# VectorE transposes that write contiguously, with the token order and the head masks made afterwards by ScalarE and GpSimd

## Chip, cores and metric

One core of a Trainium2 chip runs the kernel. The metric is device time in microseconds (us), the median of the runs. Before the change the kernel took 167.43 us (two runs, 166.48 and 168.37). A profile shows one execution. Fast runs of the kernel before differ by up to 1.4% within one set of rounds, so differences of 1 or 2 us between single traces are read with care, and the experiments were timed in several rounds against the kernel before on the same chip.

Engine names in the profile: PE is TensorE's matmul part, DVE is VectorE, ACT is ScalarE, POOL is GpSimd, SP issues DMAs. L203 is line 203 of that kernel's source; the changed kernel has other line numbers.

## The reference

A chunked linear attention (state space) layer is followed by a gated feed-forward network (FFN). What matters here, per batch entry and head:

```python
cum = np.cumsum(log(a))                    # decay
y_t = sum_{s<=t} (C_t . B_s) * exp(cum_t - cum_s) * x_s
# shapes: x (4, 8, 768, 32), a (4, 8, 768), B and C (4, 8, 768, 16)
X = y.transpose(0, 2, 1, 3).reshape(3072, 256)
out = (maximum(X @ w_gate, 0) * (X @ w_val)) @ w_out     # w: 256x1536, 256x1536, 1536x256
```

The kernel folds the decay into B and C: C is multiplied by a running product, B by its inverse. TensorE then needs the scaled B and C with the state dimension on the partitions and the tokens along the free axis. They arrive the other way round, so they have to be transposed.

## The kernel before

A batch entry has 768 tokens, split as 32 rows `r` of `K = 24` tokens. Partition p holds four groups (`q`) of 32 rows. Two heads (`t = 0, 1`) share a group, 16 state values each. The load puts B and C as `[(q r), t, (k n)]`, so a VectorE transpose of 32x32 blocks turns, for each k, the rows r into 32 columns. Token number is `24 r + k`, so the 32 columns of one block belong 24 elements apart. The kernel writes them there straight from the transpose:

```python
BT = [glob.tile([128, S], BF16) for b in range(NB)]
CT = [glob.tile([128, 2, S], BF16) for b in range(NB)]
bq = [glob.tile([128, K, 2 * N], BF16) for b in range(NB)]
cq = [glob.tile([128, K, 2, 2 * N], BF16) for b in range(NB)]   # C once per head, the other head zero

def turn_b(b, k0=0, k1=K):
    nc.vector.transpose(BT[b].rearrange("p (r k) -> p k r", k=K)[:, k0:k1], bq[b][:, k0:k1])

def turn_c(b, t, k0=0, k1=K):
    nc.vector.transpose(CT[b][:, t].rearrange("p (r k) -> p k r", k=K)[:, k0:k1],
                        cq[b][:, k0:k1, t])
```

Batch entry 0 is prepared in the start, before any FFN work. Entries 1, 2 and 3 are prepared inside FFN blocks 0, 1 and 2, between the products of the FFN (a block is 512 tokens, 12 slices f of the FFN width; the first four are done in two halves, `gvh`):

```python
for f in range(4, NF):
    gv(b, f)            # 4 matmuls, relu on ScalarE -> r, h = r * val on VectorE
    ... prep(step)      # steps 0, 1: scale B and C on GpSimd
                        # steps 2..4: turn_b in thirds;  5..10: turn_c in thirds, two heads
# after gv: state products, then fout (y @ w_out) in four quarters, with G = C.B of the next pair between
```

In the traces every engine takes its instructions in the order of the program. Six PSUM banks are shared by the FFN products and G, and a `gv` takes two of them, so PE can run about three slices ahead of VectorE.

Of the kernel before, what the change touches and what calls it, by code (L numbers as in the profile page):

```python
# [9 lines left out]
BF16 = mybir.dt.bfloat16  # L10
AF = mybir.ActivationFunctionType
ALU = mybir.AluOpType
# [17 lines left out]
def kernel(  # L30
# [13 lines left out]
    nc = tc.nc  # L44

    NB, NH, S, D = x.shape
    N = B.shape[-1]
# [7 lines left out]
    R = 32  # L55
    K = S // R
# [3 lines left out]
    glob = ctx.enter_context(tc.tile_pool(name="glob", bufs=1))  # L60
# [7 lines left out]
    def bank(name="bank", shape=(128, 512), dtype=FP32):  # L68
        return mm.tile(list(shape), dtype, tag="shared", bufs=NSHARED, name=name)
# [4 lines left out]
    def load_rows(src, b, q, name):  # L74
        rows = glob.tile([128, 2, K * N], FP32, name="%s%d" % (name, b))
        q.dma_start(out=rows, in_=src[b].rearrange("(t q) (r k) n -> (q r) t (k n)", t=2, r=R))
        return rows
# [12 lines left out]
    rows = {}  # L90
# [21 lines left out]
    tmask = const.tile([128, 2], FP32)  # L112
# [23 lines left out]
    def weights(f0, f1):  # L136
        fs = slice(f0 * 128, f1 * 128)
        for w, src in ((wg, moe_w_gate), (wv, moe_w_val)):
            nc.gpsimd.dma_start(
                out=w[:, :, fs], in_=src[:, fs].rearrange("(k p) f -> p k f", k=2))  # L140
# [8 lines left out]
    def wait_for(j, cell):  # L149
        nc.gpsimd.tensor_copy(gate[:, j:j + 1], cell)  # L150


    FC = const.tile([128, 2 * NB, K], FP32)
    FB = const.tile([128, 2 * NB, K], FP32)
# [20 lines left out]
    def inverse(b):  # L175
        nc.vector.reciprocal(FB[:, 2 * b:2 * b + 2], FC[:, 2 * b:2 * b + 2])
# [3 lines left out]

    BT = [glob.tile([128, S], BF16, name="BT%d" % b) for b in range(NB)]
    CT = [glob.tile([128, 2, S], BF16, name="CT%d" % b) for b in range(NB)]
    bq = [glob.tile([128, K, 2 * N], BF16, name="bq%d" % b) for b in range(NB)]
    cq = [glob.tile([128, K, 2, 2 * N], BF16, name="cq%d" % b) for b in range(NB)]

    def clear(b, eng):
        for t in range(2):
            eng.memset(cq[b][:, :, t, (1 - t) * N:(2 - t) * N], 0.0)

    def scale_c(b, t, eng):  # L190
        eng.tensor_tensor(
            out=cq[b][:, :, t, t * N:(t + 1) * N],
            in0=rows["C", b][:, t].rearrange("p (k n) -> p k n", n=N),
            in1=FC[:, 2 * b + t].to_broadcast([128, K, N]), op=ALU.mult)

    def scale_b(b, t, eng):
        eng.tensor_tensor(  # L197
            out=bq[b][:, :, t * N:(t + 1) * N],
            in0=rows["B", b][:, t].rearrange("p (k n) -> p k n", n=N),
            in1=FB[:, 2 * b + t].to_broadcast([128, K, N]), op=ALU.mult)  # L200

    def turn_b(b, k0=0, k1=K):
        nc.vector.transpose(BT[b].rearrange("p (r k) -> p k r", k=K)[:, k0:k1], bq[b][:, k0:k1])  # L203

    def turn_c(b, t, k0=0, k1=K):
        nc.vector.transpose(CT[b][:, t].rearrange("p (r k) -> p k r", k=K)[:, k0:k1],  # L206
                            cq[b][:, k0:k1, t])

    yT = glob.tile([128, 2, T], BF16)
    A_ps = mm.tile([128, 2, 128], FP32, tag="Aps", name="A_ps")  # L210
# [8 lines left out]
    def tokens(p, i):  # L219
        c = 2 * (p % PPB) + i  # L220
        return slice(c * 128, (c + 1) * 128)

    def rows_b(p):
        s = st[p]
        n = 1 if 2 * (p % PPB) + 1 == NC - 1 else 2
        bb = bank("bb", (128, 2, 128), BF16)
        for i in range(n):
            nc.tensor.transpose(out=bb[:, i], in_=BT[p // PPB][:, tokens(p, i)], identity=ident)
        bt = att.tile([128, 2, 128], BF16, tag="bt", name="bt")
        nc.scalar.copy(out=bt[:, 0:n], in_=bb[:, 0:n])  # L230
        s["B"] = [bt[:, i] for i in range(n)]

    def G(p):
        s = st[p]
        b = p // PPB
        g = [bank("g%d" % q, (128, 2, 2, 128)) for q in range(4)]
        for i in range(2):
            for q in range(4):
                r = slice(32 * q, 32 * q + 32)
                nc.tensor.matmul(  # L240
                    out=g[q][:, i], lhsT=BT[b][r, tokens(p, i)], rhs=CT[b][r, :, tokens(p, i)],
                    start=(i == 0), stop=True, tile_position=(32 * q, 0),
                    skip_group_check=True)
        s["gp"] = g
        s["gs"] = att.tile([128, 4, 4, 128], BF16, tag="gs", name="gs", bufs=2)
# [75 lines left out]
    def yevac(p, eng):  # L321
        s = st.pop(p)
        dst = yT[:, :, p * 256:(p + 1) * 256]
        src = s["y"].rearrange("r t i m -> r t (i m)")
        if eng is nc.scalar:
            eng.copy(out=dst, in_=src)  # L326
        else:
            eng.tensor_copy(dst, src)
# [59 lines left out]

    factors(0, 2)
    inverse(0)  # L390
    clear(0, nc.gpsimd)
    wait_for(0, al[0:1, 0, 1:2])
    weights(0, 4)
    scale_b(0, 0, nc.vector)
    scale_c(0, 0, nc.gpsimd)
    scale_b(0, 1, nc.vector)
    scale_c(0, 1, nc.vector)
    load_x(1, nc.sync)
    turn_b(0)
    cast_x(0, nc.scalar)  # L400
    keep_warm(10)
    rows_b(0)
    turn_c(0, 0)
    turn_c(0, 1)
    astep(0, 0)
    G(0)
    sevac(0, 0)
    gevac(0, half=False)
    wait_for(1, st[1]["xr"][0:1, 1, 0, 0:1])
# [6 lines left out]
    inter(0, 1)  # L416
    astep(0, 1)
    yevac(0, nc.scalar)
    rows_b(1)
    cast_x(1, nc.scalar)  # L420
    sevac(0, 1)

    for b in range(NBLK):
        P, Q, W = 2 * b + 2, 2 * b + 3, 2 * b + 1
        more = P < NPAIR
        for n in (P + 1, P + 2):
            if n < NPAIR:
                load_x(n, nc.sync)
        if b in (1, 2):
            for j, src in (("B", B), ("C", C)):  # L430
                rows[j, b + 1] = load_rows(src, b + 1, nc.sync, j.lower() + "r")

        def at(name, *fs):

            return more and f == fs[min(b, len(fs) - 1)]

        def prep(step):
            n = b + 1
            if n >= NB:
                return  # L440
            if step < 2:
                scale_b(n, step, nc.gpsimd)
                scale_c(n, step, nc.gpsimd)
            elif step < 5:
                k = 8 * (step - 2)
                turn_b(n, k, k + 8)
            elif step < 11:
                t, k = divmod(step - 5, 3)
                turn_c(n, t, 8 * k, 8 * k + 8)

        for f in range(4):
            gvh(b, f, 0)
            if b == 0 and f == 0:
                G(1)
                gevac(1)
                state(1, 0)
                weights(8, NF)
                wait_for(2, st[2]["xr"][0:1, 1, 0, 0:1])
                weights_out(0, NF)
                clear(1, nc.gpsimd)  # L460
            if f == (3 if b == 0 else 1):
                if b == 1:
                    state(W, 1)
                inter(W, 0)
                inter(W, 1)
                Dm(W)
                if b == 0:
                    state(1, 1)
                yevac(W, nc.scalar)
        for f in range(4):  # L470
            gvh(b, f, 1)
        for f in range(4, NF):
            if b == 0 and f == 4:
                factors(2, 8)
                for n in range(1, NB):
                    inverse(n)
            gv(b, f)
            if f == 4 and b in (1, 2):
                clear(b + 1, nc.gpsimd)
            if f in (4, 5):  # L480
                prep(f - 4)
            if f >= 6:
                prep(f - 4)
            if at("cast P", 6, 4, 4):
                cast_x(P, nc.gpsimd)
            if at("cast Q", 8, 5, 4):
                cast_x(Q, nc.gpsimd)
            if at("rows P", 7, 6, 5):
                rows_b(P)
            if at("state P0", 9, 8, 7):  # L490
                state(P, 0)
            if at("state P1", 10, 10, 9):
                state(P, 1)
            if at("rows Q", 99, 9, 8):
                rows_b(Q)
        if more:
            inter(P, 0)
            inter(P, 1)
        fout(b, 0)
        prep(8)  # L500
        foevac(b, 0)
        if more:
            G(P)
            gevac(P)
        prep(9)
        prep(10)
        if b == 0:
            rows_b(Q)
        fout(b, 1)
        foevac(b, 1)  # L510
        if more and b > 0:
            state(Q, 0)
        fout(b, 2)
        foevac(b, 2)
        if more:
            Dm(P)
            yevac(P, nc.scalar)
            G(Q)
            gevac(Q)
            state(Q, 1 if b else 0)  # L520
        fout(b, 3)
        foevac(b, 3)
# [32 lines left out]
```

## Time and profile before

| stretch (us) | what | PE's idle |
|---|---|---|
| 0 to 21.8 | start: loads, batch 0 prepared, first pair's attention | half |
| 21.8 to 52.3, 52.3 to 79.9, 79.9 to 111.0 | blocks 0, 1, 2: FFN plus preparation of batches 1, 2, 3 | 5.6 to 8.2 us each |
| 111.0 to 167.7 | blocks 3, 4, 5: FFN without preparation | none until the tail |

Blocks are cut where their first FFN matmul starts. The next lines are the engine-busy view of these stretches: for each stretch its length, then busy time and instructions of each engine, PE's granted clock (1.00 is full), and the DMA share and rate.

```profile
core 0: us, PE busy (x) PEld busy (x) DVE busy (x) ACT busy (x) POOL busy (x), PEclk, DMA share, GB/s
0.00:21.80 21.80, 11.32 (x54) 4.28 (x55) 17.95 (x37) 4.14 (x8) 7.42 (x19) 0.73 0.87 161
21.80:52.30 30.50, 22.76 (x183) 13.79 (x183) 27.02 (x48) 13.21 (x29) 10.95 (x20) 0.89 0.47 70
52.30:79.90 27.60, 22.04 (x175) 13.92 (x173) 21.20 (x32) 12.24 (x26) 6.14 (x11) 0.84 0.28 68
79.90:111.00 31.10, 22.94 (x176) 13.96 (x175) 25.43 (x40) 12.36 (x26) 8.30 (x15) 0.86 0.24 60
111.00:129.90 18.90, 18.90 (x176) 12.75 (x174) 12.32 (x24) 12.33 (x26) 1.94 (x4) 0.97 0.28 58
```

Block 3 takes 18.9 us and PE is busy in all of it. Blocks 0 to 2 take 28 to 31 us with the same FFN work. VectorE is busy for 21 to 27 us in them, and 12.3 us in block 3: the transposes of the preparation alone are 11.2 to 12.1 us of it in each of the three blocks. PE itself is busy 22.0 to 22.9 us there and 18.9 in block 3, at a granted clock of 0.84 to 0.89 against 0.97; so besides 5.6 to 8.2 us of idle time each block has 3 to 4 us in which PE is busy longer. In the start VectorE is busy for 17.95 of 21.8 us.

The groups of instructions by shape (busy us, mean ns of one, then idle time before them and its cause) show what that surplus is made of:

```profile
L206 DVE STREAM_TRANSPOSE CT<-cq 128x256 bf16<-128x256 bf16 x18 | 22.9, 1403 | 0.0
...
L203 DVE STREAM_TRANSPOSE BT<-bq 128x256 bf16<-128x256 bf16 x9 | 12.0, 1331 | 7.1 <-POOL bq L197 7.1
...
L206 DVE STREAM_TRANSPOSE CT<-cq 128x768 bf16<-128x768 bf16 x2 | 7.4, 3894 | 0.0
...
L203 DVE STREAM_TRANSPOSE BT<-bq 128x768 bf16<-128x768 bf16 x1 | 3.7, 3690 | 0.0
```

A transpose of 256 columns takes 1.33 to 1.40 us, one of 768 takes 3.7 to 3.9 us: (3690 - 1331) / 512 = 4.6 ns a column. That is over four cycles at the 0.96 GHz that the Trainium skill gives for this engine ("VectorE: DVE Perf Modes", section "Specifications"). Per batch the transposes take 11 us or more.

The chain of waits in the start (start us, duration, what) runs through them:

```profile
6.97 3.61 DVE BT L203
10.59 7.05 DVE CT L206 x2
17.68 0.62 PE g L240 x7
```

The first G matmul (`g`) waits from about 10.6 to 17.7 us for the two C transposes. In block 1 the timeline of VectorE (start, duration, instruction, and in brackets the idle time before it and its cause) shows two things:

```profile
64.48 1.35 DVE L203 STREAM_TRANSPOSE BT<-bq 128x256 bf16<-128x256 bf16 x1 [3.35 <-POOL bq L197]
65.45 0.89 DVE L345 TENSOR_TENSOR h<-r,val 128x512 bf16<-128x512 bf16 x1
66.27 1.32 DVE L203 STREAM_TRANSPOSE BT<-bq 128x256 bf16<-128x256 bf16 x1
67.21 0.90 DVE L345 TENSOR_TENSOR h<-r,val 128x512 bf16<-128x512 bf16 x1
```

and PE's timeline shows what it waits for in the meantime:

```profile
69.65 0.37 PE L276 MATMUL A_ps<-xb,bt 128*128 128x256 bf16 x1 [3.90 <-DVE Sm L284]
```

First, VectorE idles 3.35 us until GpSimd has scaled B. That scaling had itself waited 8.6 us for the B load. Second, from then on each h product (`h<-r,val`) is followed by a transpose that takes longer than the product, and PE idles 3.90 us for `Sm`, the evacuation of a state product, which stands behind them in VectorE's queue.

### The profile page before, as it was taken

To read this page: it belongs to the slowest core of one execution; us is meant where nothing else is said; L and a number is where in the kernel's file an instruction comes from. 1 tells how busy PE (TensorE), PEld (TensorE's weight loads), DVE (VectorE), ACT (ScalarE), POOL (GpSimd) and SP (SyncE) were. 2 spreads that over 40 slices of the span, in tenths; PEclk is the share of its full clock that TensorE was granted. 3 is DMA by queue.
4 is the path that set the end of the run, shared out by engine and by line. 5 is a ranking of instruction groups with operands and counts; after the bars stand their busy time and mean duration, and the time that the engine had idled before them with its cause. 6 is when DMAs were issued, how large, how long until landed. Compare 5 with 4: busy or idle time off the path is not lost.

```text
span 167.7 us, 2899 instructions
## 1 busy us (share of the span) xinstructions
PE 132.6 (79%) x1062; PEld 82.3 (49%) x1062; DVE 127.3 (76%) x222; ACT 76.0 (45%) x160; POOL 38.6 (23%) x73
## 2 busy tenths in 40 slices
PE   6810797881959974399894696499999999999992
PEld 2300255331637732167661245377467846786481
DVE  6999557999985746999881999947866778468821
ACT  3100285541224863015682223338745875388610
POOL 7300447460204036002308202301003210220000
PEclk9965569998795999659999579969999999999999
DMA  5999287930010950001590000109002500120012
GB/s 164 203 182 253 35 124 103 170 47 0 0 66 30 173 175 0 0 4 65 110 240 28 0 0 0 65 32 160 0 0 68 121 4 4 37 88 4 0 51 74
DMA packets 34685, 12.07 MB, mean 72 GB/s; under 512 B 26480, under 2 KB 34672, under 8 KB 34672
## 3 DMA queue, kind: packets, MB, share of 16 engines
q1 hardware_dynamic: 29888, 8.75, 23.2%
q0 software_dynamic: 3184, 2.36, 10.2%
q10 hardware_dynamic: 1600, 0.79, 1.7%
q8 instruction: 8, 0.13, 0.3%
q14 instruction: 5, 0.04, 0.1%
HBM read 11.11 MB, written 3.15 MB: 85 GB/s over the span
## 4 chain that ended last, share of the span: by engine, by line
PE 45%; DVE 27%; POOL 8%; DMA 7%; issue 6%; SPq 3%; ACT 2%; POOLq 0%; DVEq 0%; ACTq 0%
PE o L368 15%; DVE CT L206 13%; PE gate L338 7%; PE gv L356 7%; PE val L341 7%; DVE BT L203 5%; DMA br<-in_B_dram 5%; DVE h L345 4%; SPq L84 3%; POOL bq L197 2%; PE g L240 2%; PE y L313 2%; PE A_ps L276 2%; DMA al<-in_a_dram 1%; PE w L128 1%
## 5 line engine op out<-in xcount | busy, mean ns | idle before, releaser
L344 ACT ACTIVATE r<-gate 128x512 bf16<-128x512 f32 x48 | 28.7, 598 | 26.1 <-PE gate L338 22.0
L368 PE MATMUL o<-wo,h 128*128 128x256 bf16 x288 | 39.2, 294 | 1.5 <-DVE h L345 1.5
L345 DVE TENSOR_TENSOR h<-r,val 128x512 bf16<-128x512 bf16 x48 | 34.8, 728 | 5.4 <-ACT r L344 5.4
L368 PEld LDWEIGHTS <-h 128*128 128x128 bf16 x288 | 29.3, 104 | 10.0 <-issue 3.2
L338 PE MATMUL gate<-yT,wg 128*128 128x512 bf16 x96 | 30.4, 400 | 0.6 <-DVE h L345 0.6
L206 DVE STREAM_TRANSPOSE CT<-cq 128x256 bf16<-128x256 bf16 (+1 forms) x20 | 30.4, 1652 | 0.0
L341 PE MATMUL val<-yT,wv 128*128 128x512 bf16 x96 | 30.2, 398 | 0.1
L247 POOL TENSOR_SCALAR_AFFINE_SELECT gs<-gs 128x512 bf16<-128x512 bf16 (+1 forms) x24 | 12.2, 531 | 76.9 <-ACT gs L258 76.9
L360 DVE TENSOR_TENSOR h<-r,gv 128x256 bf16<-128x256 bf16 x48 | 19.9, 421 | 11.4 <-ACT r L359 10.9
L203 DVE STREAM_TRANSPOSE BT<-bq 128x256 bf16<-128x256 bf16 (+1 forms) x10 | 15.7, 1567 | 7.1 <-POOL bq L197 7.1
L264 DVE TENSOR_TENSOR gs<-g,maskUT 128x512 bf16<-128x512 f32 x24 | 16.0, 710 | 6.3 <-PE g L240 3.2
L359 ACT ACTIVATE r<-gv 128x256 bf16<-128x256 f32 x48 | 18.5, 384 | 3.8 <-PE gv L356 1.7
L356 PE MATMUL gv<-yT,wg 128*128 128x256 bf16 x96 | 19.6, 288 | 0.7 <-ACT yT L326 0.7
L356 PE MATMUL gv<-yT,wv 128*128 128x256 bf16 x96 | 19.3, 285 | 0.0
L338 PEld LDWEIGHTS <-wg 128*128 128x128 bf16 x96 | 9.4, 101 | 19.5 <-issue 12.7
L258 ACT CAST gs<-g 128x512 bf16<-128x512 f32 x12 | 7.0, 587 | 25.4 <-PE g L240 25.3
L341 PEld LDWEIGHTS <-wv 128*128 128x128 bf16 x96 | 9.8, 102 | 12.9 <-issue 2.6
L276 PE MATMUL A_ps<-xb,bt 128*128 128x256 bf16 x20 | 6.2, 310 | 12.2 <-DVE Sm L284 7.3
L326 ACT CAST yT<-y 128x512 bf16<-128x512 f32 x12 | 7.0, 586 | 11.2 <-PE y L313 9.3
L284 DVE TENSOR_TENSOR Sm<-A_ps,smask 128x256 bf16<-128x256 f32 x20 | 10.1, 503 | 1.8 <-PE A_ps L276 1.8
L240 PE MATMUL g<-CT,BT 32*128 32x256 bf16 x96 | 5.2, 296 | 7.8 <-DVE CT L206 7.8
L356 PEld LDWEIGHTS <-wg 128*128 128x128 bf16 x96 | 9.5, 104 | 2.9 <-issue 1.1
(59 smaller groups left out, 108.2 us busy)
## 6 DMA issues: line engine op xcount, KB each, us to landing
xr<-in_x_dram SPq DMA_DIRECT2D x23, 128.0 KB, 3.7
out_dram<-ob SPq DMA_DIRECT2D x10, 256.0 KB, 2.2
cr<-in_C_dram SPq DMA_DIRECT2D x4, 384.0 KB, 4.7
br<-in_B_dram SPq DMA_DIRECT2D x3, 384.0 KB, 4.3
wg<-in_moe_w_gate_dram POOLq DMA_DIRECT2D x3, 256.0 KB, 4.9
wv<-in_moe_w_val_dram POOLq DMA_DIRECT2D x3, 256.0 KB, 5.5
wo<-in_moe_w_out_dram POOLq DMA_DIRECT2D x1, 768.0 KB, 9.2
br<-in_B_dram ACTq DMA_DIRECT2D x1, 384.0 KB, 3.3
```

The costliest lines, as they stand in the source:

```text
L203: nc.vector.transpose(BT[b].rearrange("p (r k) -> p k r", k=K)[:, k0:k1], bq[b][:, k0:k1])
L206: nc.vector.transpose(CT[b][:, t].rearrange("p (r k) -> p k r", k=K)[:, k0:k1], cq[b][:, k0:k1, t])
L247: nc.gpsimd.affine_select(out=dst, in_=dst, pattern=[[0, n], [1, 128]], compare_op=ALU.is_ge, fill=0.0, base=0, channel_multiplier=-1)
L264: nc.vector.tensor_tensor(out=d[:, q], in0=g[q], in1=m, op=ALU.mult)
L338: nc.tensor.matmul(out=g, lhsT=wg[:, k, fs], rhs=yT[:, k, tk], start=(k == 0), stop=(k == 1))
L341: nc.tensor.matmul(out=v, lhsT=wv[:, k, fs], rhs=yT[:, k, tk], start=(k == 0), stop=(k == 1))
L344: nc.scalar.activation(r, g, AF.Relu)
L345: nc.vector.tensor_tensor(out=fst[b][:, f], in0=r, in1=v, op=ALU.mult)
L356: nc.tensor.matmul(out=gv_[:, j], lhsT=w[:, k, fs], rhs=yT[:, k, tk], start=(k == 0), stop=(k == 1), skip_group_check=True)
L359: nc.scalar.activation(r, gv_[:, 0], AF.Relu)
L360: nc.vector.tensor_tensor(out=fst[b][:, f, u * 256:(u + 1) * 256], in0=r, in1=gv_[:, 1], op=ALU.mult)
L368: nc.tensor.matmul(out=o[:, ts % 2], lhsT=fst[b][:, f, ts * 128:(ts + 1) * 128], rhs=wo[:, f], start=(f == 0), stop=(f == NF - 1), skip_gr ...
```

## The change

The intent: let the transpose write contiguously, and pay for the token order with cheaper strided *reads* on engines that have time. C is turned once for both heads. The head mask (a 0/1 value per partition) is multiplied in by the instruction that orders the tokens, so the zero padding and its memsets go. The core of the diff, cut at the marks:

```diff
-    bq = [glob.tile([128, K, 2 * N], BF16, name="bq%d" % b) for b in range(NB)]
-    cq = [glob.tile([128, K, 2, 2 * N], BF16, name="cq%d" % b) for b in range(NB)]
-    def turn_b / turn_c ...                       (shown above)
+    def turn(j, b):
+        tq[j, b] = glob.tile([128, K, R], BF16, name="tq%s%d" % (j, b))
+        nc.vector.transpose(tq[j, b], sq[j, b])
+
+    def span(i, b, r0, r1):
+        return tq[i, b][:, :, r0:r1].rearrange("p k r -> p r k")
+
+    def tidy_b(b, r0, r1, eng):
+        dst = BT[b][:, K * r0:K * r1].rearrange("p (r k) -> p r k", k=K)
+        (eng.copy if eng is nc.scalar else eng.tensor_copy)(out=dst, in_=span("B", b, r0, r1))
+
+    def tidy_c(b, t, r0, r1, eng):                # the same with * tmask[:, t:t+1]
 ...
+    turn("B", 0)                                  # start
+    tidy_b(0, 0, 11, nc.scalar)
+    turn("C", 0)
+    tidy_c(0, 0, 0, 11, nc.scalar)
+    tidy_c(0, 1, 0, 11, nc.vector)
 ...                                              # after the first pair's y:
+    tidy_b(0, 11, R, nc.scalar)
+    tidy_c(0, 0, 11, R, nc.scalar)
+    tidy_c(0, 1, 11, R, nc.gpsimd)
 ...
-            elif step < 11: turn_b, turn_c in thirds
+            elif step < 4:
+                turn("BC"[step - 2], n)
+            elif step < 8:
+                r = 8 * (step - 4)
+                tidy_b(n, r, r + 8, nc.scalar)
+                tidy_c(n, 0, r, r + 8, nc.scalar)
+                tidy_c(n, 1, r, r + 8, nc.gpsimd)
```

In the start the diff also puts `G(0)` ahead of the first state product. I call the `tidy` instructions ordering pieces. One of 8 rows has 8 x 24 = 192 elements per partition and reads with a step of 32 elements, 64 bytes.

## The prediction

> **What bounds the kernel now.** By the engine-busy windows, the start (0 to 21.8 us, before the first FFN matmul) and FFN blocks 0, 1, 2 (30.5, 27.6, 31.1 us) are not at PE's pace; blocks 3, 4, 5 (18.9, 18.2, 19.6 us) are. Only blocks 0 to 2 prepare B and C. In the start VectorE is busy 17.95 of 21.8 us; the chain of waits runs through the B transpose (3.61 us) and two C transposes (7.05 us). In blocks 0 to 2 nine transposes of 128x256 (1331 and 1403 ns in the groups by shape) sit between the h products; VectorE is in order, so PE runs out of PSUM banks. Blocks 1 and 2 also wait for the B load, then GpSimd's scaling: VectorE idles 3.4 and 3.5 us until 64.5 and 92.4 us. The change leaves that wait.
>
> **Costs.** Strided, 768 columns take 3.7 to 3.9 us and 256 about 1.35: 4.6 ns a column. The fp32 32x32 transposes into contiguous tiles took 0.21 to 0.24 us. The Trainium skill, "VectorE: DVE Perf Modes", section "The three transpose paths", has 311 ns for 128x128 bf16; no trace here shows that yet. Estimate for 128x768 contiguous: 0.95 us. C drops from two head-padded copies to one: per batch two transposes (1.9 us) replace 11.3 us or more.
> Added on ScalarE: per batch four B and four C pieces of 192 elements. Its copies take 0.26 us for 128 and 0.38 for 256 columns, so 0.35 us each, 0.45 with the mask, plus some penalty for the 64-byte step. On GpSimd four pieces, estimate 0.45 to 0.65 us each ("GPSIMD Engine Reference", section "Performance pitfalls for Q7 kernels": reads with a step over 8 bytes cost about half more per element; no run shows it yet). The memsets (0.42 us each) go.
>
> **On the critical path.**
> - Start: C turned at about 8.9 us, first G at 9.6 instead of 17.7: 8 us gained. The rest of batch 0's ordering (504-element pieces on ScalarE) now stands before the second pair's G: 1.5 us lost.
> - Block 0: 5 us gained.
> - Blocks 1 and 2: still wait for load, scaling, one transpose, then a serial alternation on ScalarE of relu and two ordering pieces per f (about 1.35 us an f, over PE's 0.86). I place their gains at 2.2 and 5.4 us.
> - Blocks 3 to 5: unchanged.
> Sum: 167.7 - 6.5 - 5 - 2.2 - 5.4 = 148.6; about 1.5 more for strided-read penalties: 150.
>
> **Predicted: 150 us, 80% range 144 to 157.** Faster by over 2%: 0.96; within 2%: 0.03; slower: 0.01.
>
> **What would show it.** Transposes fall from about 46 to about 8 us, near 0.95 us each. First G near 9.6 us. VectorE's total near 90 us, ScalarE's about 87, GpSimd's about 43. Blocks 0 to 2 near 25 us, still above the later ones. In blocks 1 and 2 GpSimd's wait for the B load stays, and ScalarE's relus wait for transposes and ordering pieces.
>
> **What would make it wrong.** Strided 2-byte reads could cost ScalarE 1.5 ns or more a column: each piece doubles and the time nears 156. A bf16 transpose may not run at one column per cycle. If ScalarE's pieces hide better than I think, or fewer idle gaps keep PE's granted clock up (0.84 to 0.89 in blocks 0 to 2, 0.97 to 1.0 later), it is nearer 144. Weights and x loads, now wanted 6 to 8 us earlier, might be late: the DMA share is 0.87 in the start.

## The result and the profile after

The changed kernel took 148.77 us (two runs, 148.6 and 148.94), ratio 0.8886 to the kernel before, 95% interval 0.8666 to 0.9105. Run again later in four runs it took 149.54 us, ratio 0.8911 (0.8817 to 0.9006); one of the four, 150.51 us, counts as slow, and without it the median is 149.52. A ratio is the mean time of one kernel's fast runs over that of the other's in the same rounds, so it is not quite the ratio of the medians.

The engine-busy view after, cut at the same places of the program, with the same columns:

```profile
0.00:14.92 14.92, 9.56 (x55) 3.94 (x56) 9.87 (x37) 6.38 (x11) 7.94 (x18) 0.90 1.06 205
14.92:40.48 25.56, 21.73 (x185) 13.33 (x185) 17.83 (x39) 17.37 (x38) 13.66 (x20) 0.92 0.69 102
40.48:64.98 24.50, 20.32 (x174) 13.09 (x173) 15.26 (x30) 15.72 (x34) 9.90 (x15) 0.93 0.31 76
64.98:91.22 26.24, 20.53 (x175) 12.88 (x174) 14.81 (x29) 15.80 (x34) 10.14 (x15) 0.93 0.29 71
91.22:109.60 18.38, 18.33 (x177) 12.55 (x176) 13.11 (x27) 12.14 (x26) 3.31 (x8) 1.00 0.28 59
```

| stretch | before | after | gained | predicted gain |
|---|---|---|---|---|
| start | 21.8 | 14.9 | 6.9 | 6.5 |
| block 0 | 30.5 | 25.6 | 4.9 | 5 |
| block 1 | 27.6 | 24.5 | 3.1 | 2.2 |
| block 2 | 31.1 | 26.2 | 4.9 | 5.4 |
| blocks 3 to 5 | 56.7 | 56.0 | 0.7 | 0 |

These gains sum to 20.5 us, where the medians differ by 18.7: the trace of before is of a long execution. PE's granted clock in blocks 0 to 2 was 0.84 to 0.89 and is now 0.92 to 0.93, and with the same matmuls PE's busy time fell from 132.6 to 124.8 us. How much of the gain came through the clock was not tested. The groups by shape after:

```profile
L211 POOL TENSOR_SCALAR CT<-tqC,tmask 128x192 bf16<-128x192 bf16 x12 | 11.0, 928 | 4.2 <-DVE tqC L197 4.2
...
L209 ACT ACTIVATE CT<-tqC,tmask 128x192 bf16<-128x192 bf16 x12 | 7.5, 626 | 2.8 <-DVE tqC L197 2.8
...
L204 ACT COPY BT<-tqB 128x192 bf16<-128x192 bf16 x12 | 6.2, 516 | 5.3 <-DVE tqB L197 5.3
...
L197 DVE STREAM_TRANSPOSE tqB<-sqB 128x768 bf16<-128x768 bf16 x4 | 3.9, 975 | 9.4 <-POOL sqB L190 9.4
L197 DVE STREAM_TRANSPOSE tqC<-sqC 128x768 bf16<-128x768 bf16 x4 | 3.8, 952 | 0.0
```

A transpose of 768 columns takes 0.95 to 0.98 us, a quarter of before. In exchange the ordering pieces have appeared: per batch four of each kind, 0.52 and 0.63 us on ScalarE and 0.93 us on GpSimd. VectorE's total fell from 127.3 to 94.1 us, ScalarE's rose from 76.0 to 89.2, GpSimd's from 38.6 to 48.5.

In the start the two transposes on VectorE now stand back to back:

```profile
6.78 0.96 DVE L197 STREAM_TRANSPOSE tqB<-sqB 128x768 bf16<-128x768 bf16 x1
7.67 0.93 DVE L197 STREAM_TRANSPOSE tqC<-sqC 128x768 bf16<-128x768 bf16 x1
```

and PE's timeline has the first G soon after, where it was at 17.68 us:

```profile
9.45 0.40 PE L244 MATMUL g<-CT,BT 32*128 32x256 bf16 x8 [0.69 <-ACT CT L209]
```

In block 1 it is now ScalarE's timeline that shows the pace:

```profile
53.18 0.52 ACT L204 COPY BT<-tqB 128x192 bf16<-128x192 bf16 x1 [3.75 <-DVE tqB L197]
54.64 0.62 ACT L209 ACTIVATE CT<-tqC,tmask 128x192 bf16<-128x192 bf16 x1 [0.94 <-DVE tqC L197]
55.16 0.58 ACT L348 ACTIVATE r<-gate 128x512 bf16<-128x512 f32 x1
55.64 0.52 ACT L204 COPY BT<-tqB 128x192 bf16<-128x192 bf16 x1
56.05 0.63 ACT L209 ACTIVATE CT<-tqC,tmask 128x192 bf16<-128x192 bf16 x1
```

ScalarE waits 3.75 us for the B transpose, which waits for GpSimd's scaling, which waits for the load, as before. PE is held by the same load in a second way:

```profile
51.39 0.27 PE L280 MATMUL A_ps<-xb,bt 128*128 128x256 bf16 x1 [2.16 <-POOL xb L219]
```

The cast of x (`xb`) stands behind the scaling of B and C in GpSimd's queue, so PE waits 2.16 us for it in block 1, and 4.10 us in block 2. Then ScalarE alternates a relu (`r<-gate`) with two pieces. From the C piece at 54.64 to the next at 56.05 one slice takes 1.41 us, where PE needs 0.86 for its four matmuls.

### The profile page after: what moved, and what is told of

The parts are those of the page before. It is cut to its first block, busy times and chain, and to the rows that moved or that the text cites. A ratio compares the mean times of both kernels' runs of the same rounds, so it can differ in the third digit from the quotient of the medians.

```text
span 147.2 us, 2902 instructions
## 1 busy us (share of the span) xinstructions
PE 124.8 (85%) x1056; PEld 79.2 (54%) x1062; DVE 94.1 (64%) x201; ACT 89.2 (61%) x188; POOL 48.5 (33%) x78
## 4 chain that ended last, share of the span: by engine, by line
PE 56%; DVE 10%; ACT 8%; DMA 7%; issue 7%; POOL 6%; SPq 4%; POOLq 0%; DVEq 0%; ACTq 0%
PE o L372 20%; PE gv L360 10%; PE val L345 8%; PE gate L342 8%; DMA br<-in_B_dram 6%; SPq L84 4%; POOL sqB L190 3%; PE g L244 3%; PE y L317 3%; DVE tqC L197 2%; ACT BT L204 2%; PE A_ps L280 2%; POOL xb L219 2%; ACT r L348 2%; ACT CT L209 1%
## 5 line engine op out<-in xcount | busy, mean ns | idle before, releaser
L349 DVE TENSOR_TENSOR h<-r,val 128x512 bf16<-128x512 bf16 x48 | 32.5, 681 | 10.3 <-ACT r L348 10.3
L372 PE MATMUL o<-wo,h 128*128 128x256 bf16 x288 | 36.4, 279 | 2.2 <-DVE h L349 2.1
L372 PEld LDWEIGHTS <-h 128*128 128x128 bf16 x288 | 28.0, 100 | 8.2 <-DVE h L349 3.3
L345 PE MATMUL val<-yT,wv 128*128 128x512 bf16 x96 | 29.3, 388 | 1.3 <-DVE h L349 0.8
L342 PE MATMUL gate<-yT,wg 128*128 128x512 bf16 x90 | 28.2, 390 | 0.6 <-DVE h L349 0.6
L360 PE MATMUL gv<-yT,wv 128*128 128x256 bf16 x96 | 19.1, 282 | 0.0
L345 PEld LDWEIGHTS <-wv 128*128 128x128 bf16 x96 | 9.6, 100 | 13.5 <-issue 2.9
L211 POOL TENSOR_SCALAR CT<-tqC,tmask 128x192 bf16<-128x192 bf16 (+1 forms) x13 | 13.0, 1010 | 4.2 <-DVE tqC L197 4.2
L204 ACT COPY BT<-tqB 128x192 bf16<-128x192 bf16 (+2 forms) x14 | 7.9, 562 | 9.7 <-DVE tqB L197 9.7
L190 POOL TENSOR_TENSOR sqB<-br,FB 128x384 bf16<-128x384 f32 x6 | 5.0, 837 | 20.0 <-DMA br<-in_B_dram 15.5
L209 ACT ACTIVATE CT<-tqC,tmask 128x192 bf16<-128x192 bf16 (+2 forms) x14 | 9.4, 672 | 3.0 <-DVE tqC L197 3.0
L360 PEld LDWEIGHTS <-wv 128*128 128x128 bf16 x96 | 9.8, 102 | 1.5
```

The lines of the kernel that those rows point to most:

```text
L209: eng.mul(dst, span("C", b, r0, r1), tmask[:, t:t + 1])
L211: eng.tensor_scalar_mul(dst, span("C", b, r0, r1), tmask[:, t:t + 1])
L342: nc.tensor.matmul(out=g, lhsT=wg[:, k, fs], rhs=yT[:, k, tk], start=(k == 0), stop=(k == 1))
L345: nc.tensor.matmul(out=v, lhsT=wv[:, k, fs], rhs=yT[:, k, tk], start=(k == 0), stop=(k == 1))
L349: nc.vector.tensor_tensor(out=fst[b][:, f], in0=r, in1=v, op=ALU.mult)
L360: nc.tensor.matmul(out=gv_[:, j], lhsT=w[:, k, fs], rhs=yT[:, k, tk], start=(k == 0), stop=(k == 1), skip_group_check=True)
```

## The experiments

The theory: the strided write is what made the transposes slow, it lay on the critical path, and what is left in blocks 0 to 2 is first a wait for loads and scaling and then ScalarE's alternation. Rivals: the gain comes from turning C once and from the dropped padding; or what is left has another cause. The table gives every timed run but the probe (5). Its stretches come from each run's trace, so they carry the noise of one run. The intervals of runs 1 and 2 exclude 1, but reach to within 2% of the kernel before, so whether they differ from it by 2% is unclear.

| run | median us | ratio to before (95%) | start | block 0 | block 1 | block 2 | rest |
|---|---|---|---|---|---|---|---|
| changed kernel, run again | 149.54 | 0.891 (0.882 to 0.901) | 13.8 | 25.6 | 24.9 | 26.2 | 56.0 |
| 1: stride back in the transpose | 170.8 | 1.026 (1.019 to 1.033) | 20.1 | 31.1 | 30.8 | 32.2 | 56.0 |
| 2: new way in the start only | 162.25 | 0.975 (0.970 to 0.981) | 14.6 | 31.9 | 27.5 | 29.6 | 56.0 |
| 3: early B and C rows | 139.56 | 0.841 (0.837 to 0.845) | 14.7 | 25.8 | 20.5 | 20.8 | 56.0 |
| 4: before, contiguous, unordered | 140.43 | 0.847 (0.841 to 0.853) | 13.3 | 22.6 | 22.6 | 24.0 | 56.0 |
| 6: early rows, use of idle time | 137.81 | 0.823 (0.815 to 0.831) | 13.7 | 25.6 | 20.5 | 20.8 | 56.0 |
| 7: early rows, B pieces on VectorE | 137.97 | 0.824 (0.816 to 0.831) | 15.1 | 25.0 | 19.8 | 20.3 | 56.0 |
| 8: all three | 134.36 | 0.808 (0.804 to 0.812) | 13.6 | 22.6 | 19.8 | 20.3 | 56.0 |
| 3 again | 139.61 | 0.841 (0.837 to 0.845) | 14.8 | 25.6 | 20.5 | 20.8 | 56.0 |

The changed kernel again, as a reference on the chip of runs 5 to 7:

> The changed kernel itself, so that it has a ratio from the same chip and rounds as the experiments beside it. All theories: 147 to 150 us, ratio to the kernel before 0.88 to 0.90.

It agrees with its first measurement. Its start took 13.8 us where the first trace of the same kernel has 14.9: that is the noise of one trace.

### 1. The stride moved back into the transposes

```diff
-        tq[j, b] = glob.tile([128, K, R], BF16, name="tq%s%d" % (j, b))
-        nc.vector.transpose(tq[j, b], sq[j, b])
+        tq[j, b] = glob.tile([128, R, K], BF16, name="tq%s%d" % (j, b))
+        nc.vector.transpose(tq[j, b].rearrange("p r k -> p k r"), sq[j, b])
 ...
-        return tq[i, b][:, :, r0:r1].rearrange("p k r -> p r k")
+        return tq[i, b][:, r0:r1, :]
```

> The changed kernel with the stride moved back into the transposes: they write every 24th element, and the ordering pieces of ScalarE, VectorE and GpSimd then read contiguously. Counts of transposes (two per batch) and of pieces stay as in the changed kernel. Theory (the stride of the transposes' write is what cost): transposes of 768 columns return from 0.96 to about 3.7 us, first G from 9.45 to about 15 us, blocks 0 to 2 each 3 to 5.5 us longer, total 161 to 169 us. Rival (the gain comes from turning C once instead of twice and from dropping the padding, the stride being secondary): total stays within 148 to 155 us. For the cost of strided reads: if the 64-byte step is what makes the ScalarE pieces dearer than my estimate, the 192-element pieces fall from 0.52 and 0.63 us to about 0.35 and 0.44, and GpSimd's from 0.93 to about 0.5; if not, they stay.

Measured: 170.8 us, 2.6% above the kernel before and a little above the range of the theory. The groups by shape of this run:

```profile
L197 DVE STREAM_TRANSPOSE tqC<-sqC 128x768 bf16<-128x768 bf16 x4 | 14.9, 3722 | 0.0
L197 DVE STREAM_TRANSPOSE tqB<-sqB 128x768 bf16<-128x768 bf16 x4 | 14.8, 3696 | 9.3 <-POOL sqB L190 9.3
...
L211 POOL TENSOR_SCALAR CT<-tqC,tmask 128x192 bf16<-128x192 bf16 x12 | 9.0, 760 | 20.3 <-DVE tqC L197 20.3
...
L209 ACT ACTIVATE CT<-tqC,tmask 128x192 bf16<-128x192 bf16 x12 | 5.5, 459 | 11.3 <-DVE tqC L197 11.3
...
L204 ACT COPY BT<-tqB 128x192 bf16<-128x192 bf16 x12 | 4.2, 348 | 13.9 <-DVE tqB L197 13.9
```

The transposes are back at 3.70 to 3.72 us, with counts, C once and no padding as in the changed kernel. So the rival falls: without contiguous writes the rest of the change is a loss. Only the start gains from turning C once (20.1 us against 21.8). In the blocks two long transposes and the ordering pieces cost more than nine short transposes did.

The run also measures the price of the strided reads. Read contiguously, a ScalarE piece takes 0.348 us (B) and 0.459 us (C with mask), a GpSimd piece 0.760 us. The 64-byte step adds 0.168, 0.167 and 0.168 us to them. For ScalarE this is what I had expected; for GpSimd I had expected about 0.5 us without the step, and that missed.

### 2. The new way in the start only

The start uses the new `turn` and `tidy`; blocks 0 to 2 keep `turn_b`, `turn_c` and the memsets of the kernel before.

> Only batch 0 (the start) is prepared in the new way; batches 1 to 3, in blocks 0 to 2, keep the strided transposes, the padded C and the memsets of the kernel before. Theory (gains of the start and of the blocks are on the critical path one after the other and add): the start's 6.9 us alone, so 160 to 161.5 us. Rival (the start's gain is given back in block 0, where loads of weights, x and rows then come late): 163 us or more.

Measured: 162.25 us, a gain of 4.1 us by the ratio. This lies between the two expectations, so the run doesn't confirm full addition and doesn't match the rival's threshold either. The trace has the start 7.2 us shorter than in the trace of before, and block 0 at 31.9 us against 30.5. There PE's pairs of 256-column matmuls took 0.59 to 0.63 us from 16.5 to 19.1 us, 4.4 us into the block, and 0.38 later; in the trace of before they are back at 0.38 to 0.41 from 1.7 us into the block. Part of the start's gain is thus given back in block 0. The rest of the gap between 4.1 us and the trace lies in the choice of traces: this one is of an execution of 161.23 us, the shortest of its four, and that of before, at 169.38 us, is longer than any of the seven runs in these rounds.

### 3. B and C rows loaded half a block earlier

```diff
-        if b in (1, 2):                            # at the head of block b
-            for j, src in (("B", B), ("C", C)):
-                rows[j, b + 1] = load_rows(src, b + 1, nc.sync, j.lower() + "r")
 ...
         fout(b, 1)
         foevac(b, 1)
+        if b in (0, 1):                            # in the second half of the block before
+            for j, src in (("B", B), ("C", C)):
+                rows[j, b + 2] = load_rows(src, b + 2, nc.sync, j.lower() + "r")
```

> The changed kernel with the B and C rows of batches 2 and 3 loaded half a block earlier, in the middle of blocks 0 and 1, and nothing else changed. Theory (blocks 1 and 2 are still held by the wait for the B load, then GpSimd's scaling, then one transpose): GpSimd's wait for the B load (8.0 and 7.5 us) mostly goes, the first scaling of blocks 1 and 2 starts 4 to 6 us earlier in the block, block 1 falls from 24.5 to about 21 us and block 2 from 26.2 to about 21.5, total 139 to 142 us. Rival (the alternation of relu and ordering pieces on ScalarE is what sets these blocks, the load wait is only in its shadow): total 146 us or more.

Measured: 139.56 us, and 139.61 when run again, inside the theory's range. GpSimd's timeline, first of the changed kernel and then of this one, shows the first scaling of batches 2 and 3 (in brackets how long GpSimd waited for the load):

```profile
48.95 0.84 POOL L190 TENSOR_TENSOR sqB<-br,FB 128x384 bf16<-128x384 f32 x1 [7.98 <-DMA br<-in_B_dram]
...
73.11 0.84 POOL L190 TENSOR_TENSOR sqB<-br,FB 128x384 bf16<-128x384 f32 x1 [7.52 <-DMA br<-in_B_dram]
```

```profile
42.65 0.84 POOL L190 TENSOR_TENSOR sqB<-br,FB 128x384 bf16<-128x384 f32 x1 [1.68 <-DMA br<-in_B_dram]
...
62.24 0.84 POOL L190 TENSOR_TENSOR sqB<-br,FB 128x384 bf16<-128x384 f32 x1 [0.69 <-DMA br<-in_B_dram]
```

The waits of 7.98 and 7.52 us shrank to 1.68 and 0.69. The scaling starts 2.2 and 1.3 us after the block's first matmul, where it started after 8.5 and 8.1 us. Blocks 1 and 2 fell to 20.5 and 20.8 us. So the load wait was on the path in both blocks, and it was not in the shadow of the ordering pieces. PE's waits of 2.16 and 4.10 us for the cast of x are gone from this trace as well, so part of the gain came through GpSimd's queue and not through the transposes; how much, the run does not separate.

### 4. The kernel before with contiguous transposes, in the wrong order on purpose

```diff
-    nc.vector.transpose(BT[b].rearrange("p (r k) -> p k r", k=K)[:, k0:k1], bq[b][:, k0:k1])
+    nc.vector.transpose(BT[b].rearrange("p (k r) -> p k r", k=K)[:, k0:k1], bq[b][:, k0:k1])
     # the same for C; and two scans take ALU.max in place of ALU.mult, so that all stays finite
```

> The kernel before with one thing changed: its transposes write contiguously, nothing puts the tokens in order afterwards, so the result is wrong on purpose (two scans take the maximum in place of the product, only so that numbers stay finite). Nine transposes of 256 columns per batch, padded C and memsets stay. Theory (stride): 256 columns take about 0.43 us instead of 1.35, 768 about 0.95, first G at about 9.8 us, total 142 to 146 us, below the changed kernel by what its ordering pieces cost, 3 to 7 us. Rival (count of transposes and padding matter as much as the stride): 152 us or more.

Measured: 140.43 us, with a wrong result. The groups by shape:

```profile
L206 DVE STREAM_TRANSPOSE CT<-cq 128x256 bf16<-128x256 bf16 x18 | 7.1, 420 | 0.0
...
L203 DVE STREAM_TRANSPOSE BT<-bq 128x256 bf16<-128x256 bf16 x9 | 3.9, 433 | 9.2 <-POOL bq L197 9.2
```

256 columns take 0.42 to 0.43 us instead of 1.33 to 1.40, with nothing else changed: still nine transposes per batch, still padded C and memsets. The rival falls a second time. Runs 1 and 4 together with the two kernels form a square:

| ratio to before | strided write | contiguous write |
|---|---|---|
| structure of before | 1 | 0.847 (unordered) |
| structure of after | 1.026 | 0.891 |

In parts of the time before, the contiguous write is worth 15% in the old structure and 13.5% in the new (1.026 - 0.891). The new structure costs 2.6% with strided writes and 4.4% with contiguous ones (0.891 - 0.847, about 7 us); the latter is what it costs to make the order right again. By stretches the traces of run 4 and of the changed kernel place it at 1.6 us in the start and 3.0, 1.9 and 2.2 us in blocks 0, 1 and 2.

### 5. A probe of strided reads and writes

Measuring instructions were appended after the last evacuation; their results are not used.

```diff
+    for s in (1, 2, 4, 8, 16, 24, 32):            # every s-th element written
+        d = big[:, 0:256 * s].rearrange("p (a b s) -> p a b s", b=32, s=s)
+        nc.vector.transpose(d[:, :, :, 0], flat)
+    ...                                            # plain copies of 192 elements, the same way
```

> The changed kernel with measuring instructions appended after its last evacuation, results unused. Transposes of 256 columns that write every s-th element, s = 1, 2, 4, 8, 16, 24, 32; copies of 192 elements by VectorE and ScalarE that write or read every s-th element, s = 1, 2, 4, 8, 32; the same reads by GpSimd with a mask multiplied in. Theory (cost follows the byte distance between written elements, growing until each write stands alone): the transpose goes from 0.43 us at s = 1 to 1.35 us at s = 24, rising on the way and flat from s = 8 or 16 on. Rival (any step but 1 costs the full 4.6 ns a column): s = 2 already takes 1.3 us. For reads: ScalarE 0.35 us at s = 1 and 0.52 at s = 32, GpSimd 0.76 and 0.93. For strided writes of VectorE's plain copy: if the slow write belongs to the store and not to the transpose, 192 elements at s = 32 take about 0.9 us; if it belongs to the transpose, about 0.4 us.

The transposes of 256 columns in the timeline, in the order s = 1, 2, 4, 8, 16, 24, 32:

```profile
149.10 0.45 DVE L534 STREAM_TRANSPOSE big<-flat 128x256 bf16<-128x256 bf16 x1
149.58 0.47 DVE L534 STREAM_TRANSPOSE big<-flat 128x256 bf16<-128x256 bf16 x1
150.09 0.75 DVE L534 STREAM_TRANSPOSE big<-flat 128x256 bf16<-128x256 bf16 x1
150.87 1.31 DVE L534 STREAM_TRANSPOSE big<-flat 128x256 bf16<-128x256 bf16 x1
152.22 1.27 DVE L534 STREAM_TRANSPOSE big<-flat 128x256 bf16<-128x256 bf16 x1
153.52 1.35 DVE L534 STREAM_TRANSPOSE big<-flat 128x256 bf16<-128x256 bf16 x1
154.90 1.29 DVE L534 STREAM_TRANSPOSE big<-flat 128x256 bf16<-128x256 bf16 x1
```

| distance of neighbours | 2 B | 4 B | 8 B | 16 B | 32 B | 48 B | 64 B |
|---|---|---|---|---|---|---|---|
| VectorE transpose, 256, write (us) | 0.45 | 0.47 | 0.75 | 1.31 | 1.27 | 1.35 | 1.29 |
| ScalarE copy, 192, write | 0.35 | 0.41 | 0.62 | 1.05 | | | 1.04 |
| VectorE copy, 192, write | 0.21 | 0.28 | 0.38 | 0.59 | | | 0.58 |
| ScalarE copy, 192, read | 0.35 | 0.35 | 0.36 | 0.53 | | | 0.52 |
| VectorE copy, 192, read | | 0.26 | 0.26 | 0.33 | | | 0.32 |
| GpSimd multiply, 192, read | 0.76 | 0.77 | 0.77 | 0.94 | | | 0.92 |

Empty cells were not run, but for VectorE's contiguous read: it began while the strided write before it still ran, and its 0.42 us can't be compared. ScalarE's copies ran beside VectorE's transposes. Their contiguous and 64-byte reads, 0.35 and 0.52 us, are those of run 1 and of the changed kernel, so no effect of this is seen there. The rival falls: a step of 2 costs the transpose next to nothing. The cost of writes grows until the elements are 16 bytes apart and is flat from there. This fits what the Trainium skill says: SBUF has 16-byte lines, and "each cross to a new line pays a penalty" ("SBUF — State Buffer", section "Specifications (TRN2)"). From 8 to 16 bytes the transpose touches 128 lines more and takes 0.56 us more, 4.4 ns a line. ScalarE's write touches 96 lines more and takes 0.43 us more, 4.5 ns a line. VectorE's copy touches 96 lines more as well and takes 0.21 us more, 2.2 ns a line.

One expectation missed. VectorE's plain strided copy took 0.58 us, neither the 0.9 nor the 0.4 that I had set for the two cases. The slow write is not peculiar to the transpose, since ScalarE has it too; why VectorE's copy pays half as much per line as its transpose, these runs don't show.

The table also says why the change reads with the step and doesn't write with it: for ScalarE a strided read of 192 elements costs 0.53 us, a strided write 1.05.

### 6. Early rows, and the start's pieces and factors in idle time

```diff
     gevac(0, half=False)
+    tidy_b(0, 11, R, nc.scalar)                    # were after yevac(0)
+    tidy_c(0, 0, 11, R, nc.scalar)
+    tidy_c(0, 1, 11, R, nc.vector)                 # was on GpSimd
 ...
     sevac(0, 1)
+    factors(2, 8)                                  # were at f == 4 of block 0
+    for n in range(1, NB):
+        inverse(n)
```

> The changed kernel with early B and C rows (as in the run with early rows), and two moves in the start: the rest of batch 0's ordering goes ahead of the first y evacuation, its second C head to VectorE in place of GpSimd, and the decay factors of batches 1 to 3 are computed before block 0 and not inside it. Theory (the 504-element pieces stand before the second G with 1.5 to 2 us, and block 0 waits for the factors, then GpSimd's scaling): the second G starts at about 14 us instead of 15.7, GpSimd's scaling of batch 1 at about 20 us instead of 25.4, block 0 falls from 25.8 to 22 or 23 us, total 134 to 137 us. Rival (these pieces ran in the shadow of loads and of ScalarE's chain of relu and ordering): total 138.5 us or more.

Measured: 137.81 us, between the two. The moves did what they should: the second G came at 14.25 us, the scaling of batch 1 began at 18.88 us. Block 0 hardly shrank, though (25.6 us). PE's timeline shows a wait that I had made myself, and then pairs of 256-column matmuls at 0.63 us where they take 0.38 at full clock; below it is the engine-busy line of 20 to 22 us:

```profile
18.34 0.28 PE L306 MATMUL y<-CT,Sm 128*128 128x128 bf16 x2 [1.15 <-DVE Sm L288]
...
20.46 0.63 PE L360 MATMUL gv<-yT,wg 128*128 128x256 bf16 x2
```

```profile
20.00:22.00 2.00, 2.00 (x12) 1.36 (x10) 0.45 (x2) 0.77 (x2) 2.00 (x3) 0.50 1.25 205
```

The factors (13.5 to 16.2 us on VectorE) stood ahead of the first h product and the state products (`Sm`), PE idled 0.58 us for h and 1.15 us for `Sm`, and soon after its granted clock was 0.50 for 2 us. That the idle gaps caused the drop is an inference from their order in time. The trial cannot separate it from other causes.

### 7. Early rows, B pieces of the blocks on VectorE

```diff
-                tidy_b(n, r, r + 8, nc.scalar)
+                tidy_b(n, r, r + 8, nc.vector)
```

> The changed kernel with early B and C rows, and in blocks 0 to 2 the B ordering pieces on VectorE in place of ScalarE. Theory (ScalarE's alternation of relu and two pieces, 1.4 us an f, sets the second half of these blocks): the alternation falls to about 1.05 us an f, each of the three blocks gains 1 to 1.5 us, total 135.5 to 137 us. Rival (the alternation is in the shadow of something else, or VectorE only takes its place in the same chain): 138.5 us or more.

Measured: 137.97 us, ratio 0.824 against 0.841 for run 3. This lies between the two expectations. The gain is there, about half as large as expected in each block: 25.0, 19.8 and 20.3 us against 25.8, 20.5 and 20.8. ScalarE's alternation was on the path. In block 1 its C pieces now follow each other after 1.00 us (50.37 to 51.37), as expected, but the blocks became shorter by 0.5 to 0.8 us and not by 1 to 1.5, so something else comes next close behind it.

### 8. All three moves, with the factors placed later

The edits of runs 3, 6 and 7, with the factors after block 0's first half:

```diff
+        if b == 0:
+            factors(2, 8)
+            for n in range(1, NB):
+                inverse(n)
         for f in range(4):
             gvh(b, f, 1)
```

> The version that the runs so far point to: early B and C rows, the B pieces of blocks 0 to 2 on VectorE, the rest of batch 0's ordering ahead of the first y evacuation, and the decay factors after block 0's first half (VectorE idles there 1.1 us) and not before its first h product, where they held the state products in the earlier try[...]. Theory (the three waits are on one chain and add): block 0 starts at about 13.7 us, ends by 36.5 to 38 us, blocks 1 and 2 take about 20 us each, total 133.5 to 136 us. Rival (the start stays bound by the order in which the loads land or by PE's half clock after idle gaps, whatever the engines do): 137 us or more.

> The run with early B and C rows again, for a ratio from the same chip and rounds. 139 to 141 us, ratio 0.835 to 0.845; if the two moves of the other run are worth what their traces suggested, it lies 3 us or more above it.

Measured: 134.36 us (133.86 to 134.63, six runs), ratio 0.808, with a correct result, inside the theory's range. On the same chip run 3 took 139.61. Block 0 fell to 22.6 us, from 25.0 in run 7 and 25.6 in run 6, and PE's granted clock was 1.00 as the mean of the whole run. This version beats both kernels: 19% below the kernel before, 9% below the changed one by the two ratios (0.808 / 0.891 = 0.907). The ordering piece on VectorE takes 0.39 us, less than on ScalarE:

```profile
L204 DVE COPY BT<-tqB 128x192 bf16<-128x192 bf16 x12 | 4.7, 393 | 0.0
```

## Why the prediction was right

The predicted time was 150 us, measured were 148.77 and 149.54.

- **What bounded the kernel.** Right. The strided transposes were on the path in the start and in blocks 0 to 2 (runs 1 and 4). One link of the argument was not as predicted: it had PE run out of PSUM banks behind the h products, but in the blocks of the trace before PE's longest waits, 3.46 us in block 0 and 3.90 in block 1, are for `Sm`, which stands behind the same transposes.
- **The cost of a contiguous transpose.** 0.95 us predicted, 0.95 to 0.98 measured. The estimate leaned on the skill's figure for 128x128 bf16 (page and section are named in the prediction) and on the short fp32 transposes; all agree with about one column per cycle ((952 - 420) / 512 = 1.04 ns, from the 768 columns of the changed kernel and the 256 of run 4).
- **First G.** 9.6 us predicted, 9.45 measured.
- **Gains by stretch.** 6.5, 5, 2.2 and 5.4 us predicted; 6.9, 4.9, 3.1 and 4.9 read from the traces. They are good to about 1 us only: two traces of the changed kernel have starts of 14.9 and 13.8 us. Run 2 warns of taking the start's part at its face value: alone it was worth 4.1 us by the ratio.
- **What stays in blocks 1 and 2.** Right: the wait for the B load (run 3) and ScalarE's alternation (run 7). The alternation was predicted at 1.35 us a slice and measured at 1.41. The prediction did not name PE's wait for the cast of x behind the scaling, nor what was left in block 0; there the chain of waits of the trace after runs through the decay factors on VectorE and GpSimd's scaling, and run 8 moved the factors and gained 2.4 us in block 0 over run 7 (with the start's pieces moved too).
- **The sizes that were off.** The GpSimd piece was put at 0.45 to 0.65 us and took 0.93, so GpSimd's total became 48.5 us and not 43. The base was at fault and not the stride: read contiguously it takes 0.76 us already (run 1). The low end of the estimate is near the causal mask, another GpSimd instruction of this kernel, which takes 0.41 us for 256 elements. In the blocks no wait of PE for a GpSimd piece shows in the trace. In the start one does: the second G waited 0.41 to 0.43 us for the GpSimd piece of 504 elements in runs 2, 3 and in the changed kernel run again. On ScalarE the base was right (0.35 and 0.46 us), and the penalty of 0.17 us for the step was named but not sized for a single piece.
- **Luck in the total.** The sum starts from 167.7 us. That is the span inside the profiled execution, which took 169.38 us, and not the median of 167.43. The span leaves out about 1.7 us of each execution, and this execution was 1.9 us longer than the median; the two nearly cancel. That the total came out this close rests partly on it.
- **What the prediction did not say.** It didn't separate the gain of contiguous writes from the cost of ordering. Run 4 does: the writes alone would have given 140.4 us, and about 7 us were given back for the order.

## What to carry to other kernels

An instruction whose time per element is several cycles is worth a look at the byte distance of what it writes: once neighbours were 16 bytes apart, VectorE's transpose took three times as long as a contiguous one (256 columns), and the step costs less in a read by an engine that has time (0.17 us in a ScalarE piece of 192 elements, 0.69 in its write). The extra instructions are not free: here they gave back about 7 us. Then look at what is waited for next: here loading B and C half a block earlier gained another 8 to 10 us (0.891 to 0.841 by the ratios, 149.54 to 139.56 us by the medians) that the faster transposes alone could not reach. When work is moved into another engine's queue, count the pace of that queue per loop slice, and don't put it ahead of a short instruction that TensorE is waiting for.

## What the Trainium skill lacked or had wrong

- "SBUF — State Buffer", section "Specifications (TRN2)", asks for at least two hits per 16-byte line for full bandwidth. GpSimd's reads agree (0.77 us at 8 bytes, two per line; 0.94 at 16, one per line), and so do ScalarE's (0.36 and 0.53). Writes need more: with two elements per line the transpose takes 0.75 us against 0.45, and ScalarE's copy 0.62 against 0.35. Four per line were enough for the transpose (0.47 us). VectorE's copy paid already there (0.28 against 0.21). The page gives no size of the penalty; these writes show 4.4 to 4.5 ns per line for the transpose and for ScalarE, 2.2 ns for VectorE's copy.
- "VectorE: DVE Perf Modes", section "The three transpose paths", gives one figure for the transpose and doesn't mention the layout of its destination. Writing every 24th element took 1.35 us for 256 columns, contiguous 0.45.
- "ScalarE: Activation LUTs", section "What ACT_TABLE_LOAD costs", gives 186 ns + 0.833 ns per element and about 93 ns for a pointer operand. Run 1 agrees: 0.348 us for 192 elements (0.346 by the formula) and 0.459 with the mask (0.439). No page says that a 64-byte step adds 0.17 us to a read of 192 elements and 0.69 us to a write.
- "GPSIMD Engine Reference", section "Performance pitfalls for Q7 kernels", has about 1.9 cycles per element, and 2.9 when the step is over 8 bytes. The threshold and the difference agree (+0.17 us for 192 elements is 1.05 cycles each at the page's 1.2 GHz). The level doesn't for this instruction: contiguous pieces of 192 and 504 elements took 0.760 and 1.568 us in run 1, which is 2.6 ns or 3.1 cycles per element, and about 0.26 us fixed.
